# Weight conversion on pairs of half chunks, k's maximum through TensorE, and a second batch whose q takes the block route

## The chip, the cores and the metric

The kernel runs on one core of a Trainium2 chip. A core has a matrix engine (TensorE, PE in the profile, its weight loads PEld), three element engines (VectorE = DVE, ScalarE = ACT, GpSimd = POOL) and SyncE (SP), which here only issues DMAs. Each engine works through its own list of instructions in order and waits on semaphores. PE writes to a small accumulator memory, PSUM, of eight banks; everything else lies in SBUF. The metric is the time of one execution in microseconds (us). Before the change the median of three runs is 912.94 us.

## The reference

```python
q_s = exp(q - max(q, axis=-1));  q_s /= sum(q_s, axis=-1) + 1e-9     # softmax over the 64 features
k_s = exp(k - max(k, axis=2));   k_s /= sum(k_s, axis=2) + 1e-9      # softmax over the 576 positions
kv  = einsum('bhsd,bhse->bhde', k_s, v)
out = einsum('bhsd,bhde->bhse', q_s, kv)                             # (8, 8, 576, 64)
x   = out.transpose(0, 2, 1, 3).reshape(4608, 512)
h   = maximum(x @ w_in, 0)                                           # w_in 512 x 2048
return (h * h) @ w_out                                               # w_out 2048 x 512
```

q, k, v are f32, and w_in and w_out are f64, eight bytes a word. [...]

## The kernel before, in words

**Tiles.** The eight batches have 576 positions each: 512 (the rows) and 64 (the tail). The feed-forward part runs over nine tiles of 512 rows, t = 0 to 8: one for the rows of each batch, and one for the eight tails together. While tile t is computed, the attention of batch t + 1 is made between its matmuls (`step`, `step_after`). Attention goes by pairs of heads, p = 0 to 3.

**Feed-forward.** The hidden 2048 columns go in chunks f = 0 to 15. `first` is x times w_in for one chunk (12 matmuls of 512 columns: every operand is split into a high and a low fp32r part, and three of the four products are kept), then ACT's relu `r` and a DVE product into the bank `h`; `split_g` makes `gh` (ACT) and `gl` (DVE) of h squared; `second` adds the chunk's share of the result into four banks `acc`, two chunks later. Two banks hold `h`, so the h of chunk f + 2 waits for `gl` of chunk f.

**Weights.** `load_words` brings a chunk's words of w_in and of w_out (two half chunks, 512 KB each). `scale_words` is two ACT passes in place, on the words' high and low halves; `join_words` shifts the high half left by three, puts the sign bit back and adds the low half; `split_words` rounds to the high part (ACT) and subtracts (POOL) for the low part. Before the change each half chunk goes alone: the shift writes a PSUM bank `up`, the sign step reads that bank, and the last addition is on DVE for w_in and on POOL for w_out. `convert` is called once for each half chunk; all of this happens at the start and during tile 0.

**Attention of batch 0** ("the head" below) stands in front of tile 0 as a pipeline of stages over p. k's maximum over positions: `k_max` reduces the pair's four row groups on DVE (`km`), `k_turn_max` turns the 128x128 result on PE (`kmT`), reduces it (`kc`), and spreads it by a diagonal (`dg`) and a matmul with ones (`kmb`), and `k_shift` subtracts it. q goes row-wise: `q_max`, `q_exp`, `q_norm`, then `q_turn` on PE. `kv_product` makes and splits the pair's 128x128 block matrix, and `x_product` gives x.

**Later batches.** For b below TB = 2 the same route is taken; from b = 2 on q is loaded in 32x32 blocks (`load_q_blocks`) and turned by a DVE transpose (`blocks_max`, `blocks_exp`, `blocks_norm`, `blocks_turn`, `blocks_split`), with halves of the sums exchanged by small DMAs (`swap_halves`).

**What sets the order.** Up to the end of tile 0 a scheduler orders each engine's list by its own estimate of times, SP's list too. From t = 1 on the code's order is kept (`manual_schedule`).

## Time and profile before

| | |
|---|---|
| Runs | 912.48, 912.94, 913.93 us (median 912.94) |
| The profiled execution | 910.61 us, of which the span from first to last instruction is 908.7 us |
| Mean granted clock of TensorE | 0.992 |
| Busy share of the span | PE 96%, PEld 79%, DVE 54%, ACT 38%, POOL 19% |
| Chain that ended last, by engine | PE 88%, ACT 3%, DMA 3%, DVE 2%, SP's queue 2% |

The busy shares are means over very different stages. The head and tile 0 take the first 157 us; the eight tiles behind them take the rest, one every 95.6 us as long as there is attention to mix in. Matmuls overlap each other in the records: one of 512 columns is listed with 0.39 us, while twelve of them follow each other in 2.72 to 2.79 us. PE's time is therefore read from the chain, which lists when a group began and how long until the next.

### The profile page before, as it was taken

Reading aid. Unit: us, or ns where it says so; the run is one execution under the profiler, and the core shown is the slowest. Engines: PE = TensorE matmul, PEld = TensorE weight load, DVE = VectorE, ACT = ScalarE, POOL = GpSimd, SP = SyncE. Lnnn points to the kernel's source line nnn. Section 1 sums busy time; section 2 is a strip of 40 time slices with the busy share of each in tenths; the row PEclk is TensorE's granted clock in tenths of the full one; section 3 lists DMA queues with packets and bytes.
Section 4 is the critical chain, followed back from the end, with each engine's and each line's share of the span. In section 5 each row is a group of like instructions: output and inputs, shape, how many; then the busy total and the mean of one; then the engine's idle time right before and its main releaser. Section 6 shows DMA issues by size and latency. Waiting matters only on the chain.

```text
span 908.7 us, 11603 instructions
## 1 busy us (share of the span) xinstructions
...
## 2 busy tenths in 40 slices
...
GB/s 247 341 389 35 39 26 85 37 38 38 56 84 38 38 48 80 48 33 36 82 42 34 38 90 38 38 37 56 84 38 38 7 92 1 1 38 10 0 1 47
DMA packets 141194, 57.84 MB, mean 64 GB/s; under 512 B 115920, under 2 KB 134352, under 8 KB 141008
## 3 DMA queue, kind: packets, MB, share of 16 engines
...
## 4 chain that ended last, share of the span: by engine, by line
PE 88%; ACT 3%; DMA 3%; DVE 2%; SPq 2%; issue 1%; POOL 1%; DVEq 0%
PE acc L571 41%; PE h L549 41%; PE kv L467 3%; PE x L504 2%; DMA raw_o<-in_moe_w_out_dram 1%; DMA v_tail<-in_v_dram 1%; DMA q<-in_q_dram 1%; SPq L117 1%; PE kv L470 1%; DMA k<-in_k_dram 1%; ACT raw_i L130 1%; SPq L224 0%; ACT raw_o L130 0%; POOL w_o L148 0%; DVE w_o L141 0%
## 5 line engine op out<-in xcount | busy, mean ns | idle before, releaser
L549 PE MATMUL h<-xh,wi 128*128 128x512 f32 x1152 | 383.7, 396 | 4.9 <-ACT wi L157 3.6
L571 PE MATMUL acc<-wo,gh 128*128 128x512 f32 x1152 | 350.2, 392 | 4.7 <-ACT gh L563 4.7
L549 PEld LDWEIGHTS h<-xh,wi 128*128 128x128 f32 x1152 | 217.2, 189 | 52.5 <-ACT wi L157 4.9
L571 PEld LDWEIGHTS acc<-wo,gh 128*128 128x128 f32 x1152 | 215.0, 188 | 53.3 <-ACT gh L563 7.5
L549 PE MATMUL h<-xl,wi 128*128 128x512 f32 x576 | 226.5, 393 | 0.2 <-DVE xl L540 0.2
L571 PE MATMUL acc<-wo,gl 128*128 128x512 f32 x576 | 217.5, 391 | 0.0
L555 DVE SCALAR_TENSOR_TENSOR h<-h,r 128x512 f32<-128x512 f32 x144 | 99.6, 692 | 129.0 <-ACT r L554 128.9
L564 DVE TENSOR_TENSOR gl<-h,gh 128x512 fp32r<-128x512 f32 x144 | 99.2, 689 | 117.1 <-ACT gh L563 114.8
L554 ACT ACTIVATE r<-h 128x512 f32<-128x512 f32 x144 | 85.5, 594 | 162.2 <-PE h L549 162.1
L563 ACT ACTIVATE gh<-r 128x512 fp32r<-128x512 f32 x144 | 90.7, 630 | 126.2 <-PE acc L571 125.3
L549 PEld LDWEIGHTS h<-xl,wi 128*128 128x128 f32 x576 | 109.0, 189 | 22.6 <-DVE xl L540 0.5
L571 PEld LDWEIGHTS acc<-wo,gl 128*128 128x128 f32 x576 | 108.0, 188 | 23.4
L377 POOL TENSOR_TENSOR k<-k,kmx 128x512 f32<-128x512 f32 x24 | 30.8, 1283 | 172.9 <-issue 122.2
L389 POOL PARTITION_ALL_REDUCE kmx<-km x24 | 17.4, 725 | 198.5 <-DVE km L367 156.0
L328 POOL TENSOR_TENSOR ql<-qT,qh 128x576 fp32r<-128x576 f32 x24 | 34.1, 1420 | 102.1 <-issue 53.8
L300 ACT ACTIVATE q<-q 128x576 f32<-128x576 f32 x24 | 16.5, 686 | 86.6 <-DVE q L297 84.8
L308 DVE SCALAR_TENSOR_TENSOR bsm<-bsm,sw_s 128x18 f32<-128x18 f32 x24 | 4.3, 178 | 62.1 <-DMA sw_s<-bsm 62.1
L467 PEld LDWEIGHTS kv<-v,ek 128*128 128x128 f32 x256 | 34.3, 196 | 2.5 <-ACT ek L418 0.2
L363 DVE TENSOR_REDUCE km<-k 128x128 f32<-128x512 f32 x32 | 33.9, 1060 | 2.1 <-DMA k<-in_k_dram 2.1
L467 PE MATMUL kv<-v,ek 128*128 128x129 f32 x256 | 34.8, 279 | 0.0
L327 ACT CAST qh<-qT 128x576 fp32r<-128x576 f32 x24 | 16.2, 674 | 39.7 <-DVE qT L320 39.7
L296 DVE TENSOR_TENSOR bmx<-bmx,sw_m 128x18 f32<-128x18 f32 x24 | 4.2, 176 | 44.5 <-DMA sw_m<-bmx 44.5
...
## 6 DMA issues: line engine op xcount, KB each, us to landing
...
sw_m<-bmx SPq DMA_DIRECT2D x96, 2.2 KB, 1.7
sw_s<-bsm SPq DMA_DIRECT2D x96, 2.2 KB, 1.7
```

The costliest lines, as they stand in the source:

```text
L328: nc.gpsimd.tensor_tensor(out=ql, in0=qt, in1=qh, op=ALU.subtract)
L363: nc.vector.tensor_reduce(out=km.rearrange("p (h d) -> p h d", h=2), in_=kr.rearrange("p h c d -> p h d c"), op=ALU.max, axis=AX.X,)
L377: eng.tensor_tensor(out=kr, in0=kr, in1=kmx.rearrange("p (h d) -> p h d", h=2).unsqueeze(2).broadcast_to([P, 2, C, D]), op=ALU.subtract,)
L389: nc.gpsimd.partition_all_reduce(kmx, km, channels=P, reduce_op=RED.max)
L467: nc.tensor.matmul(out=ps[:, 0:W], lhsT=kr[:, c, :], rhs=vr[:, c, :], start=(c == 0), stop=False)
L504: nc.tensor.matmul(out=ps[:, 0:SH], lhsT=a, rhs=c[:, cs], start=(j == 0), stop=(j == 2))
L549: nc.tensor.matmul(out=ps, lhsT=w[f][:, p * P:(p + 1) * P], rhs=m, start=(n == 0), stop=(n == 3 * NP - 1))
L554: nc.scalar.activation(out=r, in_=ps, func=AF.Relu)
L555: nc.vector.scalar_tensor_tensor(out=ps, in0=ps, scalar=0.0, in1=r, op0=ALU.max, op1=ALU.mult)
L563: nc.scalar.activation(out=gh, in_=r, func=AF.Square)
L564: nc.vector.tensor_tensor(out=gl, in0=ps, in1=gh, op=ALU.subtract)
L571: nc.tensor.matmul(out=acc[c], lhsT=a[:, cs], rhs=w[f], start=(f == 0 and n == 0), stop=(f == NF - 1 and n == 2),)
```

## The change

- **Weights.** Words come as 16 chunks of two halves each, in the order in which they are needed: chunk 0 is (w_in 0, w_in 1), chunk m is (w_in m+1, w_out m-1), the last is (w_out 14, w_out 15). The scale, shift, sign and rounding instructions handle a whole chunk of 128x1024; only the last addition (one half on DVE, the other on POOL) and the subtraction (two on POOL) still go by halves. The shift's result and the joined word now lie in one SBUF tile `w` of a pool with two buffers instead of a PSUM bank.
- **k's maximum, batches 0 and 1.** PE turns the raw k (four 128x128 transposes into a bank) and DVE reduces the bank of 512 in one instruction; `k_max` is gone there. The tail's maximum is turned once for a batch. The diagonal is made by ACT. k is loaded with its four row groups outermost.
- **kv.** The block matrix is scaled by ACT straight into its high part (two 64x64 blocks of a tile zeroed once) and DVE makes the low part in one instruction a block. This holds for all batches.
- **Batch 1's q** takes the block route (TB = 1), with the halves exchanged by POOL copies instead of DMAs, and the shift and the normalisation on POOL. Batch 0's tail q has its shift and normalisation on POOL.
- **Order.** SP's list keeps the code's order up to the end of tile 0 (the scheduler orders the other engines). Batch 1's 16 steps run 6 for every 5 chunks. Six weight chunks are loaded ahead of tile 0, two of them early, and one more behind each f; `convert` is called twice in the head and once for each f.

```diff
-    LW = 2
-    LD = 6
+    EARLY = 2
+    AHEAD = 6
-    TB = 2
+    TB = 1
-    cvt = ctx.enter_context(tc.tile_pool(name="cvt", bufs=4))
+    cvt = ctx.enter_context(tc.tile_pool(name="cvt", bufs=2))
...
+    halves = [("i", f) for f in range(LA)]
+    for f in range(NF):
+        halves += [("i", f + LA)] * (f + LA < NF) + [("o", f)]
...
     def scale_words(m):
...
         nc.scalar.mul(out=hi, in_=hi, mul=2.0**-112)
-        nc.scalar.mul(out=lo_i, in_=lo, mul=2.0**-29)
+        nc.scalar.mul(out=words(m, I32, 0), in_=words(m, U32, 0), mul=2.0**-29)
     def join_words(m):
-        w = cvt.tile([P, M], I32, tag="w", name=f"w_{name}{f}")
-        ps = bank(f"up_{name}{f}").bitcast(I32)
+        lo, hi = words(m, I32, 0), words(m, I32, 1)
+        w = cvt.tile([P, 2 * M], I32, tag="w", name=f"w_{m}")
         nc.vector.tensor_scalar(
-            out=ps, in0=hi, scalar1=3, scalar2=None, op0=ALU.logical_shift_left
+            out=w, in0=hi, scalar1=3, scalar2=None, op0=ALU.logical_shift_left
         )
         nc.vector.scalar_tensor_tensor(
-            out=ps if name == "i" else w, in0=hi, scalar=-(2**31), in1=ps,
-            op0=ALU.bitwise_and, op1=ALU.bitwise_or,
-        )
-        if name == "i":
-            nc.vector.tensor_tensor(out=w, in0=ps, in1=lo, op=ALU.add)
-        else:
-            nc.gpsimd.tensor_tensor(out=w, in0=w, in1=lo, op=ALU.add)
+            out=w, in0=hi, scalar=-(2**31), in1=w, op0=ALU.bitwise_and, op1=ALU.bitwise_or
+        )
+        for h, eng in enumerate((nc.vector, nc.gpsimd)):
+            at = slice(h * M, (h + 1) * M)
+            eng.tensor_tensor(out=w[:, at], in0=w[:, at], in1=lo[:, at], op=ALU.add)
     def split_words(m):
...
+        nc.scalar.copy(out=parts[:, :, 0, :], in_=w)
+        for h, (name, _) in enumerate(halves[2 * m:2 * m + 2]):
+            hi, lo = parts[:, h, 0, :], parts[:, h, 1, :]
+            nc.gpsimd.tensor_tensor(out=lo, in0=w[:, h, :], in1=hi, op=ALU.subtract)
...
     def k_turn_max(b, p):
+        for c in range(C):
+            nc.tensor.transpose(
+                out=ps[:, c * P:(c + 1) * P], in_=kr[:, c, :], identity=ident
+            )
-        nc.vector.tensor_reduce(out=kc, in_=ps[:, 0:P], op=ALU.max, axis=AX.X)
+        nc.vector.tensor_reduce(out=kc, in_=ps, op=ALU.max, axis=AX.X)
...
+        nc.vector.tensor_tensor(
+            out=kc, in0=kc, in1=made["ktm", b][:, at:at + 1], op=ALU.max
+        )
-        nc.vector.tensor_scalar(
-            out=dg, in0=ident, scalar1=kc, scalar2=None, op0=ALU.mult
-        )
+        nc.scalar.activation(out=dg, in_=ident, func=AF.Copy, scale=kc)
...
     def kv_product(b, p):
+        for at, of in blocks:
+            nc.scalar.activation(out=kvh[at, at], in_=ps[at, of], func=AF.Copy, scale=ks[at])
+        for at, of in blocks:
             nc.vector.scalar_tensor_tensor(
...
+                out=kvl[at, at], in0=ps[at, of], scalar=ks[at], in1=kvh[at, at],
+                op0=ALU.mult, op1=ALU.subtract,
+            )
...
     def swap_halves(b, t, name):
+                if b == 1:
+                    nc.gpsimd.tensor_copy(out=o[at:at + Q], in_=t[of:of + Q])
...
     def blocks_exp(b, p):
+        eng = nc.gpsimd if b == 1 else nc.vector
...
+    order.enter_context(tc.manual_schedule(engines={mybir.EngineType.SP}))
...
         for f in range(NF):
             h = first(t, f, x)
...
+            while t == 0 and steps < NF and steps * 5 < (f + 1) * 6:
+                step(b, steps)
+                step_after(b, steps, x_next)
+                steps += 1
+            if t == 0:
+                convert()
...
+            if t == 0:
+                load_words(1)
```

What the scheduler makes of it shows in each engine's list. In the rows below the first number behind a name of the weights (`raw_8`, `w8`, `raw_i6`, `wo5`) is the chunk, behind `h`, `r`, `gh`, `gl` come tile and chunk, behind q, k and what belongs to them batch and pair; the last number only tells buffers apart. In the changed kernel every line number behind 122 has moved; L149, L152 and L157 are `join_words`, L166 and L169 `split_words`, L586 is `first`'s product and L595 `gl`.

VectorE's list in the middle of tile 0, from the product of chunk 4 on, before:

```order
L555 SCALAR_TENSOR_TENSOR h_0_4_819<-h_0_4_819,r_0_4_832 128x512
L138 TENSOR_SCALAR up_o5_812<-raw_o5_392 128x512
L141 SCALAR_TENSOR_TENSOR w_o5_811<-raw_o5_392,up_o5_812 128x512
L363 TENSOR_REDUCE km_1_1_803<-k_1_1_637 128x128
L138 TENSOR_SCALAR up_i6_842<-raw_i6_554 128x512
L367 TENSOR_TENSOR km_1_1_803<-km_1_1_803,kt_1_364 64x128
L564 TENSOR_TENSOR gl_0_4_875<-h_0_4_819,gh_0_4_874 128x512
L141 SCALAR_TENSOR_TENSOR up_i6_842<-raw_i6_554,up_i6_842 128x512
L264 TENSOR_REDUCE mx_1_2_1102<-q_1_2_943 128x8
L146 ISA w_i6_841<-raw_i6_554,up_i6_842 128x1024
L555 SCALAR_TENSOR_TENSOR h_0_5_895<-h_0_5_895,r_0_5_908 128x512
```

and of the changed kernel, from the same product on:

```order
L586 SCALAR_TENSOR_TENSOR h_0_4_782<-h_0_4_782,r_0_4_795 128x512
L149 TENSOR_SCALAR w_8_974<-raw_8_706 128x1024
L595 TENSOR_TENSOR gl_0_4_834<-h_0_4_782,gh_0_4_833 128x512
L152 SCALAR_TENSOR_TENSOR w_8_974<-raw_8_706,w_8_974 128x1024
L336 STREAM_TRANSPOSE qT_1_1_801<-q_1_1_570 128x576
L157 ISA w_8_974<-raw_8_706,w_8_974 128x1024
L586 SCALAR_TENSOR_TENSOR h_0_5_840<-h_0_5_840,r_0_5_853 128x512
```

Between two products stand three conversion instructions instead of five, all three with operands in SBUF alone, and they belong to chunk 8, which `first` needs five chunks later. POOL's list beside them in the changed kernel, of which L157 is the addition for one half, L169 the two subtractions, and the rest batch 1's q:

```order
L157 TENSOR_TENSOR w_7_901<-w_7_901,raw_7_641 128x512
L328 TENSOR_TENSOR q_1_1_570<-q_1_1_570,bsm_1_1_738 128x576
L169 TENSOR_TENSOR w7_968<-w_7_901,w7_968 128x512 x2
L157 TENSOR_TENSOR w_8_974<-w_8_974,raw_8_706 128x512
L344 TENSOR_TENSOR ql_1_1_857<-qT_1_1_801,qh_1_1_856 128x576
L169 TENSOR_TENSOR w8_1026<-w_8_974,w8_1026 128x512 x2
```

Per chunk these are three additions and subtractions, as many as before, with an addition of a chunk always ahead of its two subtractions.

ScalarE's list up to the first `gh` of tile 0, before:

```order
L130 ACTIVATE raw_i6_554<-raw_i6_554 128x512
L131 ACTIVATE raw_i6_554<-raw_i6_554 128x512
L157 CAST wi2_593<-w_i2_560 128x512
L130 ACTIVATE raw_o6_556<-raw_o6_556 128x512
L131 ACTIVATE raw_o6_556<-raw_o6_556 128x512
L554 ACTIVATE r_0_0_547<-h_0_0_534 128x512
L130 ACTIVATE raw_i7_616<-raw_i7_616 128x512
L131 ACTIVATE raw_i7_616<-raw_i7_616 128x512
L157 CAST wi3_648<-w_i3_622 128x512
L563 ACTIVATE gh_0_0_550<-r_0_0_547 128x512
```

and of the changed kernel, behind the scale passes of chunk 2, which are the first after the head's last copy:

```order
L166 CAST w1_575<-w_1_486 128x2x512
L315 ACTIVATE q_1_0_375<-q_1_0_375 128x576
L143 ACTIVATE raw_3_387<-raw_3_387 128x1024
L144 ACTIVATE raw_3_387<-raw_3_387 128x1024
L585 ACTIVATE r_0_0_539<-h_0_0_526 128x512
L585 ACTIVATE r_0_1_602<-h_0_1_589 128x512
L166 CAST w2_630<-w_2_581 128x2x512
L454 ACTIVATE ek_1_0_560<-k_1_0_373 128x512
L456 ACTIVATE kt_1_370<-kt_1_370 64x128
L143 ACTIVATE raw_4_390<-raw_4_390 128x1024
L144 ACTIVATE raw_4_390<-raw_4_390 128x1024
L594 ACTIVATE gh_0_0_542<-r_0_0_539 128x512
```

The words scaled ahead of the first `gh` end with chunk 4 now; before, they ended with the halves of chunk 7.

SP's list behind the loads ahead of tile 0, before:

```order
L117 DMA raw_i15_1207<-in_moe_w_in_dram 128x4x128
L117 DMA raw_o15_1209<-in_moe_w_out_dram 128x512
L525 DMA x_tail_97<-xt_0_329 512x1x64
L197 DMA k_1_1_637<-in_k_dram 128x2x256
L224 DMA v_1_1_731<-in_v_dram 128x4x64 x2
```

and of the changed kernel:

```order
L131 DMA raw_5_393<-in_moe_w_out_dram 128x512
L556 DMA x_tail_103<-xt_0_338 512x1x64
L257 DMA v_tail_104<-in_v_dram 64x2x64 x4
L210 DMA k_1_1_568<-in_k_dram 128x8x64
L219 DMA q_1_1_570<-in_q_dram 32x18x32 x4
L126 DMA raw_6_586<-in_moe_w_in_dram 128x4x128
L131 DMA raw_6_586<-in_moe_w_out_dram 128x512
```

Before, nearly all weight loads stood ahead of batch 1's second pair; now the loads of chunk 6 and later stand behind that pair's k and q, whose buffers must be free first (q's is free once `blocks_turn` of the pair before has read it).

More of the change, by code (lines that the diff above doesn't have):

```diff
@@ L92, in attention_ffn @@
     nc.vector.memset(ones, 1.0)
-    mask = const.tile([P, P], F32, tag="mask", name="mask")
-    nc.vector.memset(mask, 0.0)
-    for j in range(2):
-        nc.vector.memset(mask[j * D:(j + 1) * D, j * D:(j + 1) * D], 1.0)
+    zeros = const.tile([P, P], F32, tag="zeros", name="zeros")
+    nc.gpsimd.memset(zeros, 0.0)
+    kv_parts = []
+    for i in range(2):
+        kv_parts.append([const.tile([P, P], F32R, tag=f"kv{c}{i}", name=f"kv{c}{i}") for c in "hl"])
+        for part in kv_parts[-1]:
+            nc.gpsimd.tensor_copy(out=part, in_=zeros)
     dram = ctx.enter_context(tc.tile_pool(name="dram", bufs=1, space=bass.MemoryType.DRAM))
@@ new lines, in attention_ffn, with load_words @@
+    for f in range(NF):
+        halves += [("i", f + LA)] * (f + LA < NF) + [("o", f)]
+    def load_words(n):
+        for m in range(len(raws), min(len(raws) + n, NF)):
+            raw = (const if m < LATE else late).tile(
+                [P, 2, M], U64, tag=f"w{m}", name=f"raw_{m}"
+            )
+            for h, (name, f) in enumerate(halves[2 * m:2 * m + 2]):
+                if name == "i":
+                    nc.sync.dma_start(
+                        out=raw[:, h, :].rearrange("p (a b) -> p a b", b=P),
+                        in_=w_in[:, f * P:(f + 1) * P].rearrange("(kc p) f -> p kc f", p=P),
+                    )
+                else:
+                    nc.sync.dma_start(out=raw[:, h, :], in_=w_out[f * P:(f + 1) * P, :])
+            raws.append(raw)
```

212 lines of the change are left out of this document (92 added, 120 removed).

## The prediction

> **What bounds the kernel now.** I read the stages first: stretches of the span with the busy time (number of instructions) of PE, PEld, DVE, ACT and POOL, the granted clock, the DMA share and GB/s. The head, tile 0, one later tile:
>
> ```profile
> 0.00:42.85 42.85, 19.83 (x98) 15.27 (x99) 38.47 (x110) 28.19 (x62) 15.40 (x31) 0.89 0.94 288
> 42.85:156.94 114.09, 106.17 (x485) 85.08 (x485) 94.43 (x173) 72.56 (x138) 68.02 (x66) 0.98 0.36 119
> 250.50:346.14 95.64, 95.64 (x450) 79.77 (x449) 52.12 (x103) 33.88 (x66) 15.72 (x21) 1.00 0.22 51
> ```
>
> The later tile is PE from end to end: 95.64 of 95.64 us. The head is DVE (38.47 of 42.85) and tile 0 takes 114.09 us for about the same PE work. The chain that ended last says who holds tile 0 (start, duration, what):
>
> ```profile
> 50.01 0.53 ACT gh L563
> ...
> 73.86 2.72 PE h L549 x12
> ...
> 90.27 0.89 PE kv L467 x8
> 91.16 0.22 PE kv L470 x2
> ...
> 94.62 0.44 PE qT L444 x4
> ...
> 113.77 1.03 DVE km L363
> ...
> 132.46 1.32 POOL w_o L148
> ...
> 156.94 6.23 PE h L549 x26
> ...
> 250.56 8.20 PE h L549 x36
> ...
> 346.14 8.20 PE h L549 x36
> ```
>
> ACT holds it at the first `gh` (50.5 us), then PE, then DVE and POOL with conversion and maxima; from 156.94 on only PE, and the tiles repeat every 346.14 − 250.56 = 95.58 us. Nothing in the change touches PE's work there, so the 751.8 us behind 156.94 stay. What can move is when tile 1 starts. This execution took 910.6 us, 2.3 below the median of 912.94; I sum against it and move the result by 2.3.
>
> **(a) The head.** DVE's groups by shape, up to 157 us (count | busy us, mean ns | idle before):
>
> ```profile
> L138 DVE TENSOR_SCALAR up_i<-raw_i 128x512 int32<-128x512 int32 x16 | 10.9, 684 | 0.1
> L363 DVE TENSOR_REDUCE km<-k 128x128 f32<-128x512 f32 x9 | 9.5, 1051 | 2.1 <-DMA k<-in_k_dram 2.1
> L264 DVE TENSOR_REDUCE mx<-q 128x8 f32<-128x512 f32 x8 | 5.4, 675 | 0.7 <-DMA q<-in_q_dram 0.7
> L400 DVE TENSOR_SCALAR dg<-ident,kc 128x128 f32<-128x128 f32 x8 | 4.4, 548 | 0.2
> L482 DVE SCALAR_TENSOR_TENSOR kv<-kv,ks,mask 128x64 f32<-128x64 f32 x16 | 3.8, 277 | 0.1
> L493 DVE TENSOR_TENSOR kvl<-kv,kvh 128x128 fp32r<-128x128 f32 x8 | 3.3, 416 | 0.0
> L367 DVE TENSOR_TENSOR km<-km,kt 64x128 f32<-64x128 f32 x9 | 3.0, 336 | 0.2
> L398 DVE TENSOR_REDUCE kc<-kmT 128x1 f32<-128x128 f32 x8 | 2.3, 285 | 1.7 <-PE kmT L396 1.6
> L512 DVE TENSOR_TENSOR xl<-x,xh 128x288 fp32r<-128x288 f32 x4 | 1.8, 442 | 0.0
> ```
>
> k's maximum costs DVE 1.051 + 0.336 + 0.285 + 0.548 = 2.22 us a pair; after, one reduce of 512 (0.675, as `mx`) and one tiny maximum (taken as 0.16): −5.5 for four pairs. kv: 2 × 0.277 + 0.416 = 0.97 becomes two block operations of 0.25: −1.9. Batch 1's part done this early (`km`, tail, q's maximum and sum) loses about 3.5. The conversion in the head takes 11 operations of 0.68 = 7.5 before; after, two chunks: shifts 2 × 0.69, sign steps 2 × 1.24, one addition 0.68: −3.0. The prices of 1024: from 442 at 288 to 684 at 512 the slope gives 1.24; the shift lies between 0.69 (it cannot cost less than its own half did) and 1.24, and I take 0.69 for a reason given under (e). `dg` goes to ACT. DVE then has 38.5 − 13.9 = 24.6 us behind 4.1, 28.7, and with 2 us of waits 30.7, the addition of chunk 0 about 1 us earlier. Behind that stand POOL's addition, ACT's copy and POOL's subtraction (1.3 + 1.1 + 1.3, rows below): the first product can run at about 33.7 instead of 42.7, −9.
>
> **(b) ScalarE up to the first `gh`.** The groups up to 157 us:
>
> ```profile
> L130 ACT ACTIVATE raw_i<-raw_i 128x512 f32<-128x512 f32 x16 | 10.9, 681 | 0.0
> L157 ACT CAST wi<-w_i 128x512 fp32r<-128x512 f32 x16 | 9.9, 618 | 4.7 <-DVE w_i L146 4.5
> L554 ACT ACTIVATE r<-h 128x512 f32<-128x512 f32 x16 | 9.5, 596 | 2.4 <-PE h L549 2.3
> L351 ACT CAST qth<-qTt 128x256 fp32r<-128x256 f32 x2 | 0.8, 377 | 1.1 <-PE qTt L344 1.1
> ```
>
> From 377 at 256 to 618 at 512 the slope gives 1.10 for a copy of 1024 and 1.16 for a scale pass. From the first product, ACT's list to `gh` of chunk 0: three chunks scaled (3 × 2.3), two copies (2.2), two relus (1.2), batch 1's exponentials and `dg` (as long as relus or shorter, 1.8), `gh` 0.6 = 12.7, with about 0.6 of waits: 47.0 against 50.5. Of the head's 9 us only 3.5 reach this point.
>
> **(c) PE behind that.** Tile 0 needs 95.6 plus three groups of turns (`qT` row, 0.44 each) = 97.0. By 47.0 it has done two products and one `kv` (2 × 2.72 + 1.11 = 6.6); 90.4 are left: 137.4 without a wait.
>
> **(d) SP.** SP's list now keeps the code's order: chunk 6's words queue behind pair 1's q, whose buffer is free when `blocks_turn` of pair 0 has run, about 53 (from 33 on POOL has twelve operations of 1.05 to 1.3 to go through, 15 us, and is held by DVE for some 5).
>
> ```profile
> L208 SPq DMA_DIRECT2D q<-in_q_dram x96: 323/496/1314, 125.0 to 691.8; - x96
> ...
> DMA to landing us min/median/max: 4.4/8.4/11.1
> ```
>
> The first row is min/median/max of one issue in ns, the second the weights' landing. 53 + 4 × 0.5 + 1 for its own issues + 4.4 = 60.5, while ACT, in order, arrives at that scale at about 56. Behind it on ACT stand the relus, and behind those DVE's products and PE; the second h bank and `second` give PE a little slack: 3 us lost (0 to 8).
>
> **(e) DVE against POOL.** All conversion operands lie in SBUF now. What the trace shows when such DVE operations meet POOL, as rows of DVE and POOL at the same time, the same `dg` without POOL beside it, then min/median/max of `up_i`, which has one operand in PSUM, and last the groups that the sum uses:
>
> ```profile
> 107.28 1.27 DVE L400 TENSOR_SCALAR dg<-ident,kc 128x128 f32<-128x128 f32 x1
> ...
> 107.20 1.27 POOL L158 TENSOR_TENSOR wi<-w_i,wi 128x512 fp32r<-128x512 f32 x1
> ...
> 6.90 0.28 DVE L400 TENSOR_SCALAR dg<-ident,kc 128x128 f32<-128x128 f32 x1
> ...
> L141 DVE SCALAR_TENSOR_TENSOR up_i<-raw_i,up_i x16: 673/684/695, 37.3 to 139.3; 128x512 int32<-128x512 int32 x16
> ...
> L148 POOL TENSOR_TENSOR w_o<-w_o,raw_o 128x512 int32<-128x512 int32 x16 | 21.1, 1316 | 20.4 <-DVE w_o L141 20.4
> L158 POOL TENSOR_TENSOR wi<-w_i,wi 128x512 fp32r<-128x512 f32 x16 | 20.6, 1290 | 5.0 <-ACT wi L157 4.8
> L277 POOL TENSOR_TENSOR qn<-q,sm 128x512 f32<-128x512 f32 x8 | 8.3, 1053 | 7.9 <-DVE sm L273 7.1 <-DVE sm L272 0.8
> L328 POOL TENSOR_TENSOR ql<-qT,qh 128x576 fp32r<-128x576 f32 x24 | 34.1, 1420 | 102.1 <-issue 53.8
> L222 POOL MEMSET v<- 128x4 f32 x9 | 0.8, 106 | 0.7 <-PE kv L467 0.7
> L555 DVE SCALAR_TENSOR_TENSOR h<-h,r 128x512 f32<-128x512 f32 x16 | 11.1, 691 | 3.2 <-ACT r L554 3.2
> ```
>
> A `dg` of 0.28 us took 1.27 when it began behind a POOL operation, and ended just after it; the 16 `up_i` never left 0.68. So operations with everything in SBUF and POOL's exclude each other, and their times add. The shift is of `dg`'s form, one tensor and all in SBUF; that it claims a path which the old form left alone is why I take its low price. [...]
>
> Per chunk: POOL 2 × 1.29 + 1.32 = 3.9, batch 1's q on POOL (two of about 1.2, one 1.42, eight tiny ones little above the 0.11 of the `v` row: 4.8 a pair, four pairs in 16 chunks) 1.2; DVE 0.55 + 1.08 + 0.55 (0.69, 1.24 and 0.69 less the overlap of about 0.15 of neighbours); less 0.14 of start-up at each of POOL's three: 6.9 us. PE needs 97.0/16 = 6.06 a chunk. Over some ten chunks the conversion sets the pace: 10 × 0.85 = 8.5 lost. Lower end 0 (pace at most 6.06), upper end below.
>
> **(f)** Tile 1's first operands now pass a slower POOL and DVE: +1 (0 to 2). New waits of small size: `kvl` behind ACT's `kvh`, hidden since `x_product` comes a stage later; without that cover 0.3 each.
>
> Sum: 137.4 + 3 + 8.5 + 1 = 149.9 instead of 156.9: −7.0, 903.6 for this execution, 905.9 on the median's scale.
>
> [...]
>
> **Rivals.**
> 1. [...] Chance 0.15.
> 2. *The shift of 1024 costs 1.24*, so that the gain of the head is eaten. The pace is then 7.4 a chunk, 5.3 more over ten, and the head 1.1 later, of which 0.5 survives: 911.7, no change. For it: the slope of the 512 rows. Against: `dg`'s behaviour. Chance 0.14.
> 3. *The other side: a blocked operation holds up the free ones behind it on DVE.* The product and `gl` (0.6 each from start to start) then no longer run beside POOL: 6.9 + 1.2 = 8.1 a chunk, 12 more: 918. It decides from 6.06 + (8.5 + 7.0)/10 = 7.6 a chunk on. For it: DVE's list is in order and has a conversion operation ahead of each product. Against: POOL's 5.1 a chunk leave gaps. Chance 0.19.
> 4. *The sign step with both inputs in SBUF runs at half speed*: 1.07 more on 14 chunks, +15: 921. The nearest rows have the same form with 18 elements, and a plain operation with two inputs:
>
> ```profile
> L308 DVE SCALAR_TENSOR_TENSOR bsm<-bsm,sw_s 128x18 f32<-128x18 f32 x24 | 4.3, 178 | 62.1 <-DMA sw_s<-bsm 62.1
> L296 DVE TENSOR_TENSOR bmx<-bmx,sw_m 128x18 f32<-128x18 f32 x24 | 4.2, 176 | 44.5 <-DMA sw_m<-bmx 44.5
> ```
>
> 178 against 176 ns, where half speed would add 18 elements of 1.08 ns, 19: against it. Chance 0.06. [...]
>
> **How the numbers follow.** The forecast (faster by 3 to 11) has 0.46. Faster: 0.46 + 0.15 = 0.61; same (within 0.2%, 1.8 us, about what a measurement tells from no change) 0.14; slower 0.19 + 0.06 = 0.25. The range 897 to 917 takes in rivals 1 and 2 and half of 3, leaving rival 4 and the worse half of 3 above and a little below. The forecast's own range is 902 to 910.
>
> **What the profile after would show.** Right: the first `h` at about 34, the first `gh` ending at 47, shifts of about 0.7 and sign steps of about 1.2 whose long ones end with a POOL operation, ACT idle once before chunk 6's scale with its words as the releaser, tile 1 starting near 150, and 95.6 us a tile from there. Wrong: a first `gh` at 50 or later (b); sign steps of 2.3 (rival 4); 8 us between products (rival 3); PE without gaps from 50 on (rival 1); shifts of 1.2 (rival 2).

## The result and the profile after

The changed kernel takes 920.95 us (920.04 to 921.68, four runs), the kernel before 913.01 in the same comparison: a ratio of 1.0092 (95% interval 1.0078 to 1.0105). It is slower by 8 us (0.9%), where 905.9 was predicted. The profiled execution of the changed kernel took 921.68 us (span 919.9), that of before 910.6 (908.7), so the two traces stand 11 us apart where the medians stand 8.

The stages, as in the prediction (busy time of PE, PEld, DVE, ACT, POOL, then clock, DMA share, GB/s): up to the first product of tile 0, from there to tile 1, and a later tile.

```profile
0.00:33.69 33.69, 22.17 (x115) 18.77 (x115) 27.06 (x74) 20.96 (x45) 16.07 (x36) 0.93 0.87 210
33.69:167.59 133.90, 111.79 (x481) 86.50 (x479) 107.98 (x147) 80.21 (x121) 100.70 (x96) 0.94 0.45 136
261.20:356.80 95.60, 95.60 (x450) 79.81 (x449) 51.27 (x99) 35.27 (x71) 15.74 (x21) 1.00 0.22 51
```

The head is some 9 us shorter: the matmuls of the first product begin at 33.69; before, two of them ran at 40.88 and the other ten from 42.66. The later tiles are the same 95.6 us. Tile 0 has become 133.9 us long, 19.8 more than the 114.1 of before. For 5.6 of these PE is busy (111.8 us against 106.2, at a granted clock of 0.94 against 0.98), for 14.2 it is idle. DVE is busy for 108 us. Pieces of the chain that ended last, in order of time:

```profile
48.44 2.22 DVE w L152
...
52.29 1.77 DVE w L149
54.13 0.60 DVE gl L595
...
66.23 7.82 DMA raw<-in_moe_w_in_dram
...
93.94 6.04 DMA raw<-in_moe_w_out_dram
...
126.28 6.89 DMA raw<-in_moe_w_out_dram
...
157.55 0.89 PE kv L501 x8
...
167.59 6.19 PE h L580 x26
```

Where before PE, DVE and POOL took turns, there are now conversion operations of 1.8 and 2.2 us and three landings of words. The conversion by groups up to 168 us, DVE's three and POOL's two, then the maximum of two single columns:

```profile
L152 DVE SCALAR_TENSOR_TENSOR w<-raw,w 128x1024 int32<-128x1024 int32 x16 | 26.6, 1659 | 0.2
L149 DVE TENSOR_SCALAR w<-raw 128x1024 int32<-128x1024 int32 x16 | 18.1, 1131 | 9.6 <-ACT raw L143 5.5 <-POOL w L169 3.7 <-POOL sw_m L297 0.3
L157 DVE CUSTOM_DVE_ANT_0 w<-raw,w 128x1024 uint16<-128x1024 uint16 x16 | 18.1, 1128 | 0.3
...
L169 POOL TENSOR_TENSOR w<-w,w 128x512 fp32r<-128x512 f32 x32 | 51.3, 1622 | 6.3 <-ACT w L166 6.0
L157 POOL TENSOR_TENSOR w<-w,raw 128x512 int32<-128x512 int32 x16 | 23.2, 1450 | 11.6 <-DVE w L152 5.1 <-ACT gh L594 1.9 <-issue 1.9
...
L433 DVE TENSOR_TENSOR kc<-kc,ktm 128x1 f32<-128x1 f32 x8 | 5.6, 703 | 0.0
...
L149 DVE TENSOR_SCALAR w<-raw x16: 630/870/1905, 25.9 to 145.1; 128x1024 int32<-128x1024 int32 x16
L152 DVE SCALAR_TENSOR_TENSOR w<-raw,w x16: 1171/1577/2327, 26.6 to 148.7; 128x1024 int32<-128x1024 int32 x16
```

The last two rows give min/median/max. Free of POOL the shift costs 0.63 to 0.69 and the sign step 1.17 to 1.24 us, as the prediction took them: 16 x (0.69 + 1.24 + 0.69) = 41.9 us of DVE instead of before's 54.6 (80 operations of 0.68). As run they take 62.8. The merging saved 13 us of DVE work, and running beside POOL put 21 on it; POOL's part rose from 62.4 to 74.5. That an operation of the one engine is drawn out while one of the other runs is called the sharing of DVE and POOL below.

One place shows what that does. DVE from the products of chunks 0 and 1 on, and what stands on the other engines (start, duration, idle before and its releaser in brackets):

```profile
44.51 1.29 DVE L586 SCALAR_TENSOR_TENSOR h<-h,r 128x512 f32<-128x512 f32 x2
46.78 0.69 DVE L149 TENSOR_SCALAR w<-raw 128x1024 int32<-128x1024 int32 x1 [0.97 <-POOL w L169]
...
48.36 2.31 DVE L152 SCALAR_TENSOR_TENSOR w<-raw,w 128x1024 int32<-128x1024 int32 x1
...
50.76 1.61 DVE L157 CUSTOM_DVE_ANT_0 w<-raw,w 128x1024 uint16<-128x1024 uint16 x1
52.29 1.77 DVE L149 TENSOR_SCALAR w<-raw 128x1024 int32<-128x1024 int32 x1
...
54.05 0.68 DVE L595 TENSOR_TENSOR gl<-h,gh 128x512 fp32r<-128x512 f32 x1
...
48.31 3.51 POOL L169 TENSOR_TENSOR w<-w,w 128x512 fp32r<-128x512 f32 x2
51.78 1.73 POOL L157 TENSOR_TENSOR w<-w,raw 128x512 int32<-128x512 int32 x1
...
48.56 1.14 ACT L594 ACTIVATE gh<-r 128x512 fp32r<-128x512 f32 x2
...
46.48 2.09 PE L501 MATMUL kv<-v,ek 128*128 128x129 f32 x8 [5.64 <-ACT ek L454]
54.78 0.50 PE L580 MATMUL h<-xh,w 128*128 128x512 f32 x1 [1.77 <-DVE gl L595]
...
60.70 1.91 DVE L149 TENSOR_SCALAR w<-raw 128x1024 int32<-128x1024 int32 x1 [1.94 <-POOL w L169]
...
63.18 1.65 DVE L152 SCALAR_TENSOR_TENSOR w<-raw,w 128x1024 int32<-128x1024 int32 x1
64.86 0.70 DVE L586 SCALAR_TENSOR_TENSOR h<-h,r 128x512 f32<-128x512 f32 x1
...
59.43 0.60 ACT L585 ACTIVATE r<-h 128x512 f32<-128x512 f32 x1
...
66.24 1.13 ACT L143 ACTIVATE raw<-raw 128x1024 f32<-128x1024 f32 x1 [5.55 <-DMA raw<-in_moe_w_out_dram]
```

`gh` of chunk 0 is ready at 49.2, but `gl`, which frees the bank for chunk 2, stands in DVE's list behind four conversion operations of later chunks. They take 6.4 us instead of 3.3: POOL's operations end at 49.58, 51.82 and 53.51, and the three long ones on DVE end 1.1, 0.55 and 0.55 us behind these, about the time that each needs alone. `gl` starts at 54.05. The product of chunk 2 is then held a second time: its relu is done at 60.03, but on DVE a later chunk's shift stands ahead of it, which waits 1.94 us for POOL's subtraction to free one of the two buffers of `w` and then takes 1.91, and a sign step of 1.65. The product of chunk 1 ends at 45.8, that of chunk 2 starts at 64.9. ACT's stop of 5.55 us at the words of chunk 6 begins at 60.69 and so belongs to the next product: the relu of chunk 3 stands behind it and runs at 68.30.

What PE waited for longest up to tile 1, in the changed kernel and before (us in total, times, longest):

```profile
PE h L580 <- DVE gl L595: 11.8, 8, 2.7
...
PE acc L571 <- ACT gh L563: 4.7, 6, 1.3
```

Before the change PE did not wait for `gl` at all.

**How the rest is read.** The start times of DVE's products show where tile 0 loses time, for every kernel that follows: the product of chunk 0, the time between chunks 0 and 1, 1 and 2, 2 and 11, 11 and 13, 13 and 15, and from 15 to the first product of tile 1. Behind that, every kernel takes 750 to 756 us to the end of its span.

| | chunk 0 | 0 to 1 | 1 to 2 | 2 to 11 | 11 to 13 | 13 to 15 | 15 to tile 1 | median us |
|---|---|---|---|---|---|---|---|---|
| before | 49.0 | 3.9 | 7.3 | 63.7 | 11.6 | 13.5 | 9.3 | 911.9 to 913.0 |
| changed | 44.5 | 0.6 | 19.7 | 60.3 | 23.0 | 12.0 | 8.8 | 920.95 |
| e1 PSUM | 48.3 | 2.5 | 4.8 | 73.9 | 17.5 | 25.2 | 5.1 | 934.28 |
| e2 words ahead | 44.5 | 0.6 | 24.3 | 59.2 | 13.1 | 11.9 | 20.6 | 928.90 |
| e4 q on DVE | 46.5 | 1.7 | 14.2 | 61.2 | 18.4 | 15.5 | 9.2 | 920.66 |
| h1 head alone | 49.1 | 3.8 | 6.9 | 62.2 | 15.2 | 14.9 | 5.6 | 910.44 |
| e7 code's order | 39.5 | 11.9 | 7.8 | 81.6 | 13.0 | 9.8 | 11.0 | 927.32 |
| e8 = e7, PSUM | 46.4 | 11.3 | 6.7 | 76.9 | 12.9 | 11.2 | 11.1 | 930.40 |
| e9 = e7, words ahead | 39.6 | 11.8 | 15.9 | 81.1 | 13.0 | 9.8 | 11.0 | 936.03 |
| e10 = e8, words ahead | 46.1 | 11.3 | 9.9 | 78.0 | 13.8 | 11.2 | 11.1 | 932.33 |
| f1 words behind v | 44.0 | 0.6 | 21.5 | 59.9 | 11.8 | 16.1 | 16.4 | 923.51 |
| f2 order of DVE | 44.0 | 0.6 | 16.9 | 61.8 | 14.3 | 22.2 | 9.2 | 922.72 |
| f3 = f1 + f2 | 44.3 | 0.6 | 16.0 | 63.8 | 12.0 | 16.1 | 15.9 | 923.79 |
| f4 = f3, PSUM | 47.4 | 2.0 | 6.6 | 69.5 | 16.4 | 29.5 | 9.0 | 933.77 |
| g1 q by rows | 44.8 | 0.6 | 15.9 | 56.7 | 17.6 | 12.9 | 15.8 | 918.72 |
| g2 = g1, words | 45.1 | 0.6 | 18.9 | 59.7 | 10.0 | 12.6 | 20.7 | 920.74 |
| g4 = g1, SP free | 43.6 | 3.6 | 10.4 | 62.5 | 12.9 | 11.0 | 23.2 | 922.11 |
| g5 two buffers | 43.8 | 0.6 | 18.8 | 66.5 | 13.8 | 13.3 | 13.4 | 926.89 |
| g6 no exchange | 46.3 | 2.4 | 14.7 | 61.8 | 18.0 | 10.2 | 9.0 | 915.10 |
| h3 = h1, SBUF | 49.8 | 1.6 | 21.2 | 71.8 | 12.3 | 12.4 | 16.3 | 939.46 |

The changed kernel is 4.5 us ahead at chunk 0 and 7.8 at chunk 1, loses 12.5 between chunks 1 and 2, wins 3.5 up to chunk 11, and loses 11.4 up to chunk 13. So there are two stalls, A (1 to 2) and B (11 to 13).

### The profile page after: what moved, and what is told of

Same layout as the page of the kernel before. It is cut to its first block, busy times and chain, and to the rows that moved or that the text cites. A ratio compares the mean times of both kernels' runs of the same rounds, so it can differ in the third digit from the quotient of the medians.

```text
span 919.9 us, 11720 instructions
## 1 busy us (share of the span) xinstructions
PE 881.0 (96%) x4038; PEld 726.1 (79%) x4038; DVE 491.1 (53%) x878; ACT 355.8 (39%) x657; POOL 210.1 (23%) x249
## 3 DMA queue, kind: packets, MB, share of 16 engines
q10 hardware_dynamic: 1712, 1.31, 0.5%
## 4 chain that ended last, share of the span: by engine, by line
PE 83%; DVE 4%; DMA 3%; POOL 3%; issue 3%; SPq 2%; ACT 1%; POOLq 0%; ACTq 0%; DVEq 0%
PE acc L602 39%; PE h L580 38%; PE kv L501 3%; PE x L535 2%; DMA raw<-in_moe_w_out_dram 1%; POOL w L169 1%; DVE w L152 1%; SPq L219 1%; DMA raw<-in_moe_w_in_dram 1%; PE kv L504 1%; POOL w L157 1%; DVE w L149 1%; DMA kt<-in_k_dram 1%; DVE w L157 0%; POOL sw_s L297 0%
## 5 line engine op out<-in xcount | busy, mean ns | idle before, releaser
L580 PE MATMUL h<-xh,w 128*128 128x512 f32 x1152 | 384.0, 397 | 12.8 <-DVE gl L595 12.4
L602 PE MATMUL acc<-w,gh 128*128 128x512 f32 x1152 | 358.7, 394 | 2.3 <-ACT gh L594 2.2
L580 PEld LDWEIGHTS h<-xh,w 128*128 128x128 f32 x1152 | 217.5, 189 | 63.8 <-DVE gl L595 16.7
L602 PEld LDWEIGHTS acc<-w,gh 128*128 128x128 f32 x1152 | 216.7, 189 | 50.2 <-ACT gh L594 4.0
L580 PE MATMUL h<-xl,w 128*128 128x512 f32 x576 | 226.7, 394 | 0.2 <-DVE xl L571 0.2
L602 PE MATMUL acc<-w,gl 128*128 128x512 f32 x576 | 223.4, 391 | 0.0
L586 DVE SCALAR_TENSOR_TENSOR h<-h,r 128x512 f32<-128x512 f32 x144 | 99.5, 692 | 124.6 <-ACT r L585 124.3
L595 DVE TENSOR_TENSOR gl<-h,gh 128x512 fp32r<-128x512 f32 x144 | 99.1, 688 | 115.7 <-ACT gh L594 112.5
L580 PEld LDWEIGHTS h<-xl,w 128*128 128x128 f32 x576 | 109.1, 189 | 22.1 <-DVE xl L571 0.5
L602 PEld LDWEIGHTS acc<-w,gl 128*128 128x128 f32 x576 | 108.2, 188 | 23.0
L169 POOL TENSOR_TENSOR w<-w,w 128x512 fp32r<-128x512 f32 x32 | 51.3, 1622 | 6.3 <-ACT w L166 6.0
L323 DVE SCALAR_TENSOR_TENSOR bsm<-bsm,sw_s 128x18 f32<-128x18 f32 x28 | 5.6, 200 | 62.0 <-DMA sw_s<-bsm 60.5
L343 ACT CAST qh<-qT 128x576 fp32r<-128x576 f32 x28 | 18.9, 674 | 46.3 <-DVE qT L336 46.3
L519 ACT ACTIVATE kvh<-kv,ks 64x64 fp32r<-64x64 f32 x64 | 19.7, 308 | 38.1 <-DVE ks L513 36.7
```

The lines of the kernel that those rows point to most:

```text
L169: nc.gpsimd.tensor_tensor(out=lo, in0=w[:, h, :], in1=hi, op=ALU.subtract)
L519: nc.scalar.activation(out=kvh[at, at], in_=ps[at, of], func=AF.Copy, scale=ks[at])
L580: nc.tensor.matmul(out=ps, lhsT=w[f][:, p * P:(p + 1) * P], rhs=m, start=(n == 0), stop=(n == 3 * NP - 1))
L586: nc.vector.scalar_tensor_tensor(out=ps, in0=ps, scalar=0.0, in1=r, op0=ALU.max, op1=ALU.mult)
L595: nc.vector.tensor_tensor(out=gl, in0=ps, in1=gh, op=ALU.subtract)
L602: nc.tensor.matmul(out=acc[c], lhsT=a[:, cs], rhs=w[f], start=(f == 0 and n == 0), stop=(f == NF - 1 and n == 2),)
```

## The experiments

In brackets behind a time stands its ratio to the kernel before, run beside it, and, where given, the 95% interval of that ratio.

**First set: one part undone each.** e1 puts the conversion back on halves through PSUM:

```diff
-        nc.vector.tensor_scalar(out=w, in0=hi, scalar1=3, ...)
-        nc.vector.scalar_tensor_tensor(out=w, in0=hi, ..., in1=w, ...)
+        for h in range(2):
+            ps = bank(f"up_{m}_{h}").bitcast(I32)
+            nc.vector.tensor_scalar(out=ps, in0=hi[:, at], scalar1=3, ...)
+            nc.vector.scalar_tensor_tensor(out=w[:, at] if h else ps, in0=hi[:, at], ..., in1=ps, ...)
+            # then one half's addition on DVE from ps, the other's on POOL
```

> The changed kernel with only join_words put back on halves through a PSUM bank, so that no conversion operation on DVE but the additions' neighbours reads two SBUF tensors. Theory L (the exclusive sharing of DVE and POOL sets tile 0's pace): sign steps never above 0.70 us and POOL's subtractions never above 1.35, tile 1 starts 8 to 10 us earlier (near 158), about 912. Theory W (the late words of chunks 6, 10 and 14 set it): the three waits of ACT on words stay at about 10 us together, tile 1 moves by under 3 us, 918 or more.

934.28 us (1.0237, 1.0223 to 1.0251). The sharing was gone, and stall A with it (4.8 us), but the time rose. The lists are laid out anew by the scheduler, and in the new ones PE's longest wait is for a subtraction that POOL makes late. DVE's sign step, POOL's subtraction, and that wait (us in total, times, longest):

```profile
L155 DVE SCALAR_TENSOR_TENSOR up<-raw,up 128x512 int32<-128x512 int32 x16 | 11.0, 689 | 0.2
L174 POOL TENSOR_TENSOR w<-w,w 128x512 fp32r<-128x512 f32 x32 | 41.1, 1306 | 18.0 <-ACT w L171 9.4 <-issue 7.3 <-DMA q<-in_q_dram 1.1
...
PE h L585 <- POOL w L174: 10.0, 1, 10.0
```

Neither theory's number came; ACT's waits on words stayed, as theory W had it (12.5 us). What holds is the mechanism: with a PSUM operand the sign step is back at 0.69 and POOL's subtraction at 1.31.

e2 loads more words ahead (`AHEAD = 12`):

> The changed kernel with twelve instead of six chunks of words loaded ahead of tile 0 (AHEAD = 12), so that only the last four stand behind a wait of SP. Theory W: ACT's waits on words fall from 10.0 us to under 3 and tile 1 starts 7 to 9 us earlier, about 913. Theory L: the waits go too, but the time is taken by the pace of DVE and POOL instead: tile 1 moves by under 3 us, 918 or more, and sign steps stay near 1.6 us.

928.90 us (1.0175, 1.0161 to 1.0189). Stall B went (13.1 us), A grew to 24.3, and tile 1 came 20.6 us behind the last product. e4 has batch 1's q on DVE (`eng = nc.vector` in `blocks_exp` and `blocks_norm`):

> The changed kernel with the shift and the normalisation of batch 1's q on DVE (0.76 us each, with two SBUF inputs) instead of POOL (1.42 and 1.58). Theory L: the time that both engines share falls by about 1.5 us a pair, 6 in all, 915. Theory W: q's turn comes earlier and with it the words behind it, 1 to 2 us at each of three chunks, 3 to 5 in all, 916 to 918, and ACT's waits on words shrink while sign steps do not. A DVE bound would show as no gain.

920.66 us, no change against 920.95: neither theory's gain came. h1 is the kernel before with the parts of the change that concern k's maximum, the diagonal and kv:

```diff
 # the kernel before, with k_tail_max, k_turn_max, kv_product, k's layout of the change
-        k_max(0, p)
+        if p == 0:
+            k_tail_max(0)
```

> The kernel before with only k's maximum through PE (batches 0 and 1), the diagonal by ACT and the kv split of the change; conversion, q and SP's order as before. Theory: DVE saves 1.4 + 0.5 us a pair, 7.5 in the head and 6 in tile 0; of the head's part some 3 reach tile 0 and of tile 0's most, so 904 to 908. Rival: the head ends on ACT's list and DMA and tile 0 on PE, 911 to 913.

910.44 us against 912.56 (0.9978, 0.9969 to 0.9987): faster by 2 us, and the only kernel here that beats the one before. The rival was nearer: the work saved on DVE does not move its product of chunk 0 at all (49.1 against 49.0). What sets it there was not tried.

**Second set: the same order for all.** Since the scheduler answers each edit with other lists, e7 keeps the code's order on all engines from tile 0 on, and the next three differ from it in one thing each:

```diff
-        if t == 1:
+        if t == 0:
             order.close()
             ctx.enter_context(tc.manual_schedule())
```

> The changed kernel with the code's order kept on all engines from tile 0 on (before: on SP alone), so that no conversion is pulled ahead of an earlier chunk's product or gl. It is the base for the next three, whose lists differ from it only in what they name. Theory O (the estimate behind the lists, which knows neither the exclusive sharing nor the late words, pulls conversions ahead of gl of chunk 0 and bunches the last ones; that is most of the loss): no stall above 9 us between two products, about 912. Rival: the costs stay wherever they stand, 918 to 925, since an order that isn't filled by estimate leaves gaps of its own.

> e7 with the conversion on halves through a PSUM bank as before the change. With the same order elsewhere this is the price of the exclusive sharing. Theory L: 13 chunks convert in tile 0, a chunk's DVE part falls from about 3.6 (0.87 + 1.58 + 1.06) to 3.4 but POOL's three from 4.5 to 3.9 and nothing blocks, so 0.5 to 0.8 a chunk, 6 to 10 us below e7. Rival: no more than 2 us, and the sharing was only where waits were put down.

> e7 with twelve chunks of words loaded ahead of tile 0. Theory W: ACT's waits on words (10 us in the changed kernel) go and the time falls by 5 to 10 us against e7. Rival: they were hidden behind the pace of DVE and POOL, within 2 us of e7.

> e7 with both. If the two costs are independent, the sum of the two differences, 11 to 18 us below e7 and faster than the kernel before (about 900 to 905). If one hides behind the other, no better than the better of the two.

927.32, 930.40, 936.03 and 932.33 us (ratios 1.0164, 1.0199, 1.0263, 1.0226). Theory O's 912 did not come. In e7 chunks 1 to 2 take 7.8 us, but 0 to 1 take 11.9: from 0 to 2 it is 19.6 us, hardly less than the 20.3 of the changed kernel, and PE waits there at batch 1's `kv` and x (2.8 us at 45.17, 3.3 at 53.92). It is slow elsewhere too (81.6 us from chunk 2 to 11), and five of its gaps between products are above 10 us. e8 against e7 is the cleanest price of the sharing: from the product of chunk 1 to that of 15, e7 takes 112.1 us and e8 107.7, so 4.4 us in tile 0, although e8 has 80 conversion operations on DVE instead of 48. In the head it is the other way: DVE's product of chunk 0 comes at 39.5 in e7 and 46.4 in e8, where PE waits 3.4 us at 37.28 for the tail's maximum on DVE and 1.9 at 41.10 for POOL's subtraction. The sum favours SBUF by 3 us. e9 failed for a reason of its own: SP issued six chunks ahead of batch 1's v tail, and PE waited for that (us in total, times, longest):

```profile
PE kv L504 <- DMA v_tail<-in_v_dram: 13.8, 1, 13.8
```

In e2 the v tail landed at 61.3 instead of 46.1, and the q of pair 2 was issued at 111.2 instead of 90.7. So e2 and e9 priced the wrong thing, and e10's sum says nothing on independence.

**Third set: the stalls one by one.** f1 loads the words behind the v tail; f2 adds one rule on DVE's list; f3 has both, f4 also e1's conversion:

```diff
     load_tail_v(1)
+    load_words(6)                                  # f1
...
-                convert()
+                with tc.issue_after(made["gl", 0, f - 1].ins):   # f2, for f > 0
+                    convert()
```

> The changed kernel with the words of chunks 6 to 11 loaded right behind batch 1's v tail, ahead of SP's first wait (in e2 and e9 they stood ahead of the v tail and delayed it by 8 to 14 us). In the changed kernel the time between the products of chunks 1 and 2 is 19.7 us and between 11 and 13 it is 23.0 (before: 7.3 and 11.6). Theory W (late words): the second falls to 13 or less, ACT's waits on words from 10 us to under 2, and the time to 908 to 913. Theory O (the order of the lists): the first stall stays or grows and takes most of it, 917 or more.

> The changed kernel with one rule for the lists: the conversion emitted in chunk f's turn is queued behind gl of chunk f-1 on DVE, so gl of chunk 0 no longer stands behind two conversions (7.3 us of DVE time in the changed kernel, with the sharing). Words as in the changed kernel. Theory O: the first stall falls from 19.7 to 12 us or less, 912 to 915. Theory W: ACT still stops for the words of chunk 6, so the stall ends where it did, 918 to 921.

> f1 and f2 together. If late words and the order explain the miss, both stalls are gone (under 12 and 13 us) and the time is that of the forecast, 900 to 908. If the exclusive sharing of DVE and POOL is the rest, the pace between the products of chunks 2 and 11 stays at 6.7 us or more and it is 909 to 914.

> f3 with the conversion on halves through a PSUM bank, so without the exclusive sharing. From e7 against e8: 4 us gained between the products of chunks 1 and 15, 7 us lost in the head, so about 3 above f3. If the sharing costs what the prediction said (8.5 us), it is below f3.

923.51, 922.72, 923.79 and 933.77 us (1.0137, 1.0119, 1.0130, 1.0241). f1 cured stall B as theory W said (23.0 to 11.8) and ACT's waits on words, and gained nothing: its product of chunk 15 stands at 153.8, 6.4 us earlier than in the changed kernel, but tile 1 follows 16.4 us later instead of 8.8. In f1, that is where batch 1's last pair is still being made:

```profile
156.88 0.68 DVE L397 TENSOR_TENSOR k<-k,kmb 128x512 f32<-128x512 f32 x1
...
163.08 0.40 PE L535 MATMUL x<-qh,kvh 128*128 128x288 f32 x1 [2.23 <-ACT kvh L519]
164.91 0.61 PE L535 MATMUL x<-qh,kvl 128*128 128x288 f32 x1 [1.30 <-DVE kvl L521]
167.61 0.80 PE L580 MATMUL h<-xh,w 128*128 128x512 f32 x1 [1.37 <-ACT xh L570]
```

With words on time x of tile 1 becomes the late one. f2 did what it was to do on DVE: `gl` of chunk 0 starts at 48.75, 5.3 us earlier, and PE's waits for `gl` fall from 11.8 to 1.2 us. Yet stall A went from 19.7 to 16.9 only. In f2, the relu of chunk 2 stands in ACT's list behind a rounding copy, which waits for the addition on DVE:

```profile
58.90 1.05 ACT L166 CAST w<-w 128x1024 fp32r<-128x1024 f32 x1 [5.98 <-DVE w L157]
59.97 0.60 ACT L585 ACTIVATE r<-h 128x512 f32<-128x512 f32 x1
```

No wait for words lies in that stretch. So a late conversion stops the chunk from ACT's list too. f3 was expected at 900 to 908 and is at 923.8: with these two edits together the loss stays. f4, expected 3 us above f3 or below it, is 10 above: PE stands for 13.9 us at one of POOL's subtractions, as in e1.

**Fourth set: batch 1's attention.** In the changed kernel its q loads, one a pair, stand 33 us apart; before, the pairs' loads stood some 25 apart (SP's rows, of the changed kernel, then of before):

```profile
57.53 1.96 SPq L219 DMA_DIRECT2D q<-in_q_dram  x4
90.69 2.26 SPq L219 DMA_DIRECT2D q<-in_q_dram  x4
123.44 2.26 SPq L219 DMA_DIRECT2D q<-in_q_dram  x4
...
49.27 1.89 SPq L197 DMA_DIRECT2D q<-in_q_dram  x1
72.75 0.38 SPq L197 DMA_DIRECT2D q<-in_q_dram  x1
97.81 0.38 SPq L197 DMA_DIRECT2D q<-in_q_dram  x1
```

g1 puts batch 1's q back on the row route, g5 gives k and q two buffers, g6 leaves the exchange of halves out for batch 1 (its softmax then uses 32 features' maximum and sum, so it is a probe and no candidate), g2 is g1 with f1's words:

```diff
-    TB = 1
+    TB = 2                                         # g1, g2, with the row route's calls in step
...
-        t = att.tile([P, NG, Q], F32, tag="q", name=f"q_{b}_{p}")
+        t = att.tile([P, NG, Q], F32, tag="q", name=f"q_{b}_{p}", bufs=2)   # g5
...
     def swap_halves(b, t, name):
+        if b == 1:                                 # g6
+            return t
```

> The changed kernel with batch 1's q on the row route of before (TB = 2), all else as changed. New theory Q: what sets the start of tile 1 is batch 1's attention, four pairs in series: q of a pair passes POOL, ACT and DVE seven times, each time behind conversions in the lists, and the next pair's q is loaded only when it is turned; its loads stand 33 us apart in the changed kernel (57.5, 90.7, 123.4) against 25 before (49.3, 72.8, 97.8). Then the loads come 24 to 28 us apart here and the time is 904 to 912. If conversion, words and order are the cause by themselves, it stays at 917 or more.

> The changed kernel with two buffers each for k and q of the later batches (and eleven instead of twelve chunks in the pool that is open from the start, for room), the same list on SP. Pair p+1's k, q and the words behind them then wait for pair p-1 only. If the single buffer makes the chain, ACT's waits on words vanish, the loads come 25 us apart and the time is 906 to 913. If the chain is long because of the lists of POOL and DVE, the loads come early but the maxima that use them don't, and it is 917 to 922.

> The changed kernel without the exchange of halves for batch 1 (its softmax then uses 32 features' maximum and sum instead of 64's), so without 32 small POOL copies and two passages through POOL a pair. Theory Q: the period of q's loads falls from 33 us by 3 to 5, tile 1 starts 8 to 16 us earlier, 905 to 913. If POOL's busy time matters and not the passages, 32 x 0.2 = 6 us at most of POOL's 93 go, and the time falls by 2 or less.

> g1 with the words of chunks 6 to 11 behind the v tail (as f1). Theory Q: with the row route the words are no longer late, within 2 us of g1. If late words are a cost of their own, 3 to 8 us below g1.

918.72, 926.89, 915.10 and 920.74 us (1.0076, 1.0163, 1.0036, 1.0099). g6 is the only edit of the changed kernel's own lists that recovered much, 5.9 us, though it ends 2 us above theory Q's 913; yet its loads still stand 33 to 37 us apart, so the period was the wrong sign to look for. The second buffer recovered nothing, and the loads of pairs 2 and 3 came no earlier (94.3 and 135.1); g5 also has one chunk of words fewer in the pool that is open from the start, for room. Nothing in it points at the single buffer as the cause. The row route gives back 2.2 us, and its loads too stay 33 us apart (83.4 and 116.4 for k). So q's route is a part, and not the main one.

**Last pair.** h3 changes one line of h1, the place of the shift's result; g4 takes SP's kept order from g1 (the line `order.enter_context(...)` left out):

```diff
-        ps = bank(f"up_{name}{f}").bitcast(I32)
+        ps = w
```

> h1 (the kernel before with k's maximum through PE and the kv split) with one thing more: the shift's result lies in SBUF instead of a PSUM bank, still half chunk by half chunk, SP's list left to the scheduler, q as before. If the conversion in SBUF is what loses the time (exclusive sharing, and lists laid out without it), it is 914 or more against h1's 910.4, with sign steps up to 1.9 us. If it gains as it did in the head of e7 against e8 (7 us earlier) and the sharing hides, 905 to 909; then SP's list and the pacing of the steps are the loss.

> g1 with SP's list left to the scheduler in the head and tile 0. If SP's kept order is what makes pairs' k and q and the words late, the loads of k come 25 to 28 us apart as in the kernel before and the time is 908 to 914. If the loads wait for the work on DVE and ACT that frees their buffers, they stay 33 us apart and the time is within 2 us of g1's 918.7.

939.46 us (1.0295, 1.0281 to 1.0309): one operand moved, and h1's 910.4 becomes 29 us longer. Groups of h3, then of h1:

```profile
L145 DVE SCALAR_TENSOR_TENSOR w_i<-raw_i,w_i 128x512 int32<-128x512 int32 x16 | 21.2, 1322 | 0.1
L150 DVE CUSTOM_DVE_ANT_0 w_i<-raw_i,w_i 128x1024 uint16<-128x1024 uint16 x16 | 19.7, 1234 | 0.2
L162 POOL TENSOR_TENSOR wo<-w_o,wo 128x512 fp32r<-128x512 f32 x16 | 27.6, 1723 | 1.5 <-ACT wo L161 1.5
...
L145 DVE SCALAR_TENSOR_TENSOR up_i<-raw_i,up_i 128x512 int32<-128x512 int32 x16 | 11.0, 686 | 0.1
L150 DVE CUSTOM_DVE_ANT_0 w_i<-raw_i,up_i 128x1024 uint16<-128x1024 uint16 x16 | 10.9, 682 | 1.1
L162 POOL TENSOR_TENSOR wo<-w_o,wo 128x512 fp32r<-128x512 f32 x16 | 20.7, 1298 | 12.0 <-ACT wo L161 12.0
```

Sign step and addition of w_in take nearly twice as long, stall A is back (21.2 us), PE waits 11.4 us for `gl` (in h1, never), and tile 1 is late too. The scheduler laid out other lists here as well, so the 29 us are not the price of the sharing alone. g4 is at 922.11 (1.0107, 1.0094 to 1.0121), 3.4 above g1, outside both of its expectations, with loads of k 40 and 32 us apart: SP's kept order is not the loss either.

**What is shown, and what isn't.** In the six kernels whose conversion goes through PSUM (before, h1, e1, f4, e8, e10) PE never waits for `gl` up to tile 1; in the fourteen with all of it in SBUF it does, for 1.1 to 11.8 us. With lists laid out by the scheduler, chunks 0 to 2 take 7.3 to 11.2 us with PSUM and 14.0 to 24.9 with SBUF. So stall A goes with where the conversion's operands lie; h3 against h1 changes that alone, with lists laid out anew, and has 21.2 against 6.9 us from chunk 1 to 2. That the conversions ahead of `gl` are all of it is not shown: f2 and f3 took them away and kept 16.9 and 16.0 us, behind ACT's rounding copy. In the code's order these chunks are slow with either (e8 18.0, e7 19.6), where PE waits at batch 1's `kv`. More than two buffers for `w` were not tried; DVE's shift waited 3.7 us in all for one (row of L149 above).

Stall B goes with late words: among the kernels with SBUF it is 10.0 to 13.1 us where ACT does not wait for words (e2, e7, e9, f1, f3, g2, g4, h3) and 13.8 to 23.0 where it does (changed, e4, f2, g1, g5, g6). That batch 1's attention is the next to be late when B is cured is shown by f1's rows; f3, g2 and g4 have the same long step from chunk 15 to tile 1. How the 8 us divide among the three stays open: an edit of one re-lays the lists, the gains don't add, and no edit of the changed kernel brought it back to the time before.

## Why the prediction was wrong, by its own steps

- **(a) The head** was right: the first product at 33.69 against 33.7, shifts of 0.63 to 0.69 and sign steps of 1.17 to 1.24 where POOL left them free. That the times agree to 0.01 us is luck: the step's own terms give 29.7 + 3.7 = 33.4, and in the trace DVE's addition ends at 29.8, ACT's copy starts 2.4 us later, behind a scale pass, and PE begins 0.9 us before the first of POOL's subtractions ends. Rival 2 (shift at 1.24) and rival 4 (sign step at half speed) are out. The 0.69 for a shift of this width and rival 4's 1.07 for half speed were the author's estimates, which no run before the change shows; what was measured are the 0.63 to 0.69 and 1.17 to 1.24 above. One price was far off: the maximum of two single columns, taken as 0.16, is 0.70 on the mean (group `kc`, x8), as it waits out POOL's operation (the one at 38.32 took 1.29 us and ended 0.02 us behind POOL's addition).
- **(b) ScalarE** was 2.2 us short: `gh` of chunk 0 ends at 49.2; 47.0 was forecast, and before it was 50.5. Behind the first product ACT stood idle for 3.1 us, where the step had 0.6.
- **(c) PE without a wait** failed first. PE waited 21.6 us between its first product and tile 1 (before, 7.6), 5.6 of them ahead of `kv` at 46.5, which the step counted as done by then, and 11.8 for `gl`. It was meant as a base to which (d) and (e) add 11.5 us; the waits were about twice that. PE's own busy time rose by 5.6 us too, which the step had at nothing.
- **(d) SP** named the mechanism and one case of three. ACT waited for words three times (5.55, 1.75 and 2.65 us, 10.0 in all), each time behind a pair's q; q of pair 1 was issued at 57.5, not 53, and chunk 6's words came to be used at 66.2, not 60.5. The step should have applied its own argument to pairs 2 and 3.
- **(e) The sharing** had the right pace and the wrong place. From chunk 2 to 11 it is 60.3/9 = 6.7 us a chunk, 6.9 was forecast; before it was 7.1, so that over these chunks nothing was lost. That the pace came so near is in part luck: its 0.15 for the overlap of neighbours and 0.14 for start-up rest on no row, and with the 0.08 and 0.04 by which neighbours on DVE and on POOL overlap in the trace of before it would have been 7.4. Its rule that operations with everything in SBUF and POOL's exclude each other is wider than the traces: the changed kernel's four transposes of q in tile 0 took 0.76 to 0.77 us each, one of them at 86.30 beside a POOL subtraction that ran until 87.54, against 0.77 to 0.78 in the kernel before. What was not priced is where late operations stand in the lists: ahead of `gl` of chunk 0 and of the product of chunk 2 on DVE (stall A, 12.5 us over before), and among the last conversions ahead of the product of chunk 13 (in B). That is the mechanism of rival 3, a blocked operation holding up free ones behind it, which was given 0.19. Its numbers came out by luck: it had 8.1 us for every chunk and 918 us; the mean over chunks 1 to 15 is 115/14 = 8.2 and the time 920.95, above even the range's upper end of 917, but that mean is made of 6.7 a chunk and two stalls, of which B comes with late words. Its objection, that POOL leaves gaps, was weak: POOL was busy for 100.7 of 133.9 us.
- **(f) The boundary** was forecast 1 us longer (0 to 2) and came 0.5 shorter: 7.4 us from the last product to tile 1, 7.9 before.

The step that failed is (e), in the way in which it enters the sum: the sharing as a rate, 8.5 us over ten chunks, added to a PE without waits, with nothing for what stands behind a blocked operation in an in-order list. In its place the runs show stops: 12.5 us lost between two products, and 11.8 us of PE's waits for `gl`, which no kernel with the conversion through PSUM has. The second is (d), with 3 us for one wait on words, where ACT waited three times, 10.0 us in all, and chunks 11 to 13 lost 11.4; f1 takes that stall away. Of the head's gain, 4.5 us were there at DVE's product of chunk 0, and at that of chunk 2 the kernel was 4.7 behind.
